# Second MLP of a linear-attention and two-MLP kernel as Strassen block products over three parts of 768 tokens

## The chip, the cores and the metric

The kernel runs on one core of a Trainium2 chip. The metric is the device time of one execution in microseconds, on that core. The time before is the median of three executions, 895.91 us (895.73 to 897.20).

## What is computed

Linear attention over 4 batches of 8 heads and 576 positions, then two MLPs over the 2304 tokens that result. The second MLP adds no bias and has no scale; its activation is Mish.

```python
def _attn_ref(q, k, v):
    q_s = softmax of q over the head dimension (64)
    k_s = softmax of k over the sequence (576)
    kv = np.einsum('bhsd,bhse->bhde', k_s, v)
    return np.einsum('bhsd,bhde->bhse', q_s, kv)

x = attention output as [2304, 512]
h = x @ w_in;  r = np.maximum(h, 0.0);  g = s * (r * r) + b;  x = g @ w_out      # first MLP, [512, 2048], [2048, 512]
h = x @ w_in;  g = h * np.tanh(softplus(h));  out = g @ w_out                    # second MLP, same sizes
```

All inputs are 32-bit floats to the reference; on the chip the four weight matrices arrive as 64-bit floats, two 32-bit words per element, and the kernel makes 32-bit floats of them with shifts and masks.

## The kernel before, in words

Every product of the MLPs is made to near 32-bit precision by three passes of the matmul unit: each operand is split into a high part (rounded to the matmul's format) and a low part (the rest), and `passes` (L177 to L185, matmul L181) adds high x high, high x low and low x high in PSUM. The high part is a copy on ACT (L174, or L160 for weights), the low part a subtraction on DVE (`minus`, L171).

The tokens are cut into five chunks of 512, 256, 512, 512 and 512 (`CHUNKS`). One *step* is one chunk and one block f of 128 of the 2048 columns: `emit_h` makes h (128 hidden columns x the chunk, 4 blocks of the 512 inputs x 3 passes = 12 matmuls), `emit_relu2` (first MLP) or `emit_mish` (second) makes g and its split, `emit_y` adds the block's share of y (12 matmuls in a chunk of 512). Steps 0 to 79 are the first MLP (called MLP1 here), steps 80 to 159 the second (MLP2), whose chunks come in the order 0, 2, 1, 3, 4. h runs two steps ahead of y in MLP1 and three in MLP2 (`LEAD`, `LEAD2`, `h_slot`). In the first MLP y lies as output columns x tokens, in the second as tokens x output columns. At the end of a chunk `y_out` scales y and stores it, in MLP1 to `y_dram` in DRAM (tile `yd`, L300) and in MLP2 to the output. `x2_load` (L215) reads a chunk back as input of MLP2, and `x_split` adds the bias term `bsum` (L205, L206).

Beside these steps run the attention of the next chunk (the `att` stages, placed by `at` at step numbers) and the conversion of the weights. A *unit* holds 1024 elements per partition: `load_w` (L112, L117) brings 1 MB of raw words in two DMAs, `conv_abs`, `conv_bits` (L137 to L151), `conv_hi` (L160) and `conv_lo` make its two halves. The units of MLP1 are converted at the start and in the first chunk; those of MLP2 from step 61 on, on the fly, into the slots that MLP1 gives up. SP issues nearly all DMAs and does so strictly in its order: a DMA that waits holds the ones behind it. The tile framework orders each engine's instructions by program order and priorities; `order` rows below show the result.

Of the kernel before, what the change touches and what calls it, by code (L numbers as in the profile page):

```python
# [26 lines left out]
def kernel(  # L27
# [169 lines left out]
    def x_split(ph, c, kk):  # L197
# [3 lines left out]
        if ph == 0:  # L201
            split(hi, lo, src)
        else:
            b = bsum[:, kk:kk + 1]
            nc.scalar.activation(out=hi, in_=src, func=AF.Identity, bias=b)  # L205
            nc.vector.scalar_tensor_tensor(  # L206
                out=lo, in0=src, scalar=b, in1=hi.bitcast(F32), op0=ALU.add, op1=ALU.subtract
            )
# [2 lines left out]
    def x2_load(c):
        n = CHUNKS[c]
        for kk in range(NK):
            t = xp.tile([P, CM], F32, tag=f"xn{kk}", name=f"x2_{c}_{kk}")
            nc.sync.dma_start(out=t[:, 0:n], in_=y_dram[c][:, kk, :])  # L215
            x_next[1, c, kk] = t[:, 0:n]
# [521 lines left out]
```

## Time and profile before

| | |
|---|---|
| median of 3 executions | 895.91 us (895.73 to 897.20) |
| profiled execution | 896.14 us |
| its span, first to last instruction | 894.4 us |
| mean granted clock of the matmul unit | 0.988 of 2.4 GHz |
| matmul unit (PE) | 859.6 us busy, 4364 matmuls, as many weight loads |
| DVE, ACT, POOL | 392.3, 389.9, 3.7 us busy |
| bytes moved by DMA | 62.59 MB |

The profiled execution is 1.74 us longer than its span, and 0.23 us above the median. An engine is busy in a stretch when one of its instructions runs; a wait is put down to the instruction whose end released it. DMA issues are not counted as busy time.

### The profile page before, as it was taken

To read this page: it belongs to the slowest core of one execution; us is meant where nothing else is said; L and a number is where in the kernel's file an instruction comes from. 1 tells how busy PE (TensorE), PEld (TensorE's weight loads), DVE (VectorE), ACT (ScalarE), POOL (GpSimd) and SP (SyncE) were. 2 spreads that over 40 slices of the span, in tenths; PEclk is the share of its full clock that TensorE was granted. 3 is DMA by queue.
4 is the path that set the end of the run, shared out by engine and by line. 5 is a ranking of instruction groups with operands and counts; after the bars stand their busy time and mean duration, and the time that the engine had idled before them with its cause. 6 is when DMAs were issued, how large, how long until landed. Compare 5 with 4: busy or idle time off the path is not lost.

```text
span 894.4 us, 11164 instructions
## 1 busy us (share of the span) xinstructions
PE 859.6 (96%) x4364; PEld 713.1 (80%) x4364; DVE 392.3 (44%) x648; ACT 389.9 (44%) x901; POOL 3.7 (0%) x26
## 2 busy tenths in 40 slices
PE   5689987999999999999999999999999999999998
PEld 3368876998788888888888888888889888888886
DVE  5999856445333444344787497211111211121111
ACT  7677656477555645444346233322122321132221
POOL 1000000000000000000000000000000000000000
PEclk9899997999999999999999999999999999999999
DMA  8982231322111011014444151010011100001001
GB/s 239 288 289 67 80 85 39 100 64 59 43 39 39 12 47 24 1 50 139 141 143 167 68 186 49 25 48 0 1 48 48 41 31 1 0 1 48 1 1 47
DMA packets 72516, 62.59 MB, mean 70 GB/s; under 512 B 39312, under 2 KB 62096, under 8 KB 72464
## 3 DMA queue, kind: packets, MB, share of 16 engines
q1 hardware_dynamic: 71376, 60.84, 21.9%
q10 hardware_dynamic: 1088, 1.05, 0.4%
q8 instruction: 34, 0.56, 0.3%
q14 instruction: 18, 0.15, 0.1%
HBM read 52.43 MB, written 9.44 MB: 69 GB/s over the span
## 4 chain that ended last, share of the span: by engine, by line
PE 90%; DMA 4%; SPq 2%; ACT 1%; DVE 1%; issue 0%; DVEq 0%; ACTq 0%
PE h L181 43%; PE y L181 43%; DMA raw<-in_moe_w_out_dram 3%; PE x L181 1%; PE kv L463 1%; DMA q<-in_q_dram 1%; PE qt L472 1%; DMA kvb<-in_k_dram 1%; SPq L112 1%; SPq L342 0%; SPq L370 0%; ACT q L428 0%; PE km L404 0%; PE km L397 0%; SPq L346 0%
## 5 line engine op out<-in xcount | busy, mean ns | idle before, releaser
L181 PE MATMUL h<-xh,w 128*128 128x512 f32 (+1 forms) x1280 | 390.7, 372 | 10.6 <-ACT w L160 5.0
L181 PEld LDWEIGHTS h<-xh,w 128*128 128x128 f32 x1280 | 235.5, 190 | 53.8 <-ACT w L160 5.6
L171 DVE TENSOR_TENSOR gl<-r,gh 128x512 fp32r<-128x512 f32 (+1 forms) x159 | 100.8, 635 | 353.2 <-ACT r L255 265.4
L181 PE MATMUL h<-xl,w 128*128 128x512 f32 (+1 forms) x640 | 237.4, 371 | 0.5 <-DVE xl L171 0.4
L181 PE MATMUL y<-gh,w 128*128 128x512 f32 (+1 forms) x640 | 196.5, 372 | 0.0
L181 PE MATMUL y<-w,gh 128*128 128x512 f32 x568 | 175.0, 390 | 0.0
L254 ACT ACTIVATE gh<-h 128x512 fp32r<-128x512 f32 (+1 forms) x79 | 43.8, 554 | 253.5 <-PE y L181 228.3
L181 PEld LDWEIGHTS h<-xl,w 128*128 128x128 f32 x640 | 121.5, 190 | 23.3 <-DVE xl L171 2.8
L181 PEld LDWEIGHTS y<-gh,w 128*128 128x128 f32 x640 | 117.4, 189 | 19.7
L181 PEld LDWEIGHTS y<-w,gh 128*128 128x128 f32 x568 | 105.6, 188 | 21.0
L181 PE MATMUL y<-gl,w 128*128 128x512 f32 (+1 forms) x320 | 119.9, 375 | 0.0
L181 PE MATMUL y<-w,gl 128*128 128x512 f32 x284 | 110.3, 389 | 0.0
L245 ACT ACTIVATE r<-h 128x512 f32<-128x512 f32 (+1 forms) x80 | 44.3, 553 | 103.9 <-PE h L181 95.7
L181 PEld LDWEIGHTS y<-gl,w 128*128 128x128 f32 x320 | 60.9, 190 | 10.6 <-DVE gl L171 0.4
L181 PEld LDWEIGHTS y<-w,gl 128*128 128x128 f32 x284 | 53.4, 188 | 11.3
L428 ACT ACTIVATE q<-q,qm 128x64 f32<-128x64 f32 x144 | 48.2, 336 | 18.1 <-DVE qm L409 17.9
L160 ACT CAST w<-t 128x1024 fp32r<-128x1024 f32 (+1 forms) x34 | 34.0, 1001 | 47.6 <-DVE t L151 46.2
L174 ACT CAST gh<-r 128x512 fp32r<-128x512 f32 (+1 forms) x80 | 46.0, 577 | 3.8 <-PE y L181 2.0
L246 ACT ACTIVATE r<-r 128x512 f32<-128x512 f32 (+1 forms) x80 | 46.8, 589 | 1.9
L255 ACT ACTIVATE r<-h 128x512 f32<-128x512 f32 (+1 forms) x80 | 44.0, 551 | 0.0
L171 DVE TENSOR_TENSOR w<-t,w 128x1024 fp32r<-128x1024 f32 (+1 forms) x34 | 39.2, 1153 | 2.9 <-ACT w L160 2.9
L151 DVE SCALAR_TENSOR_TENSOR t<-raw,t 128x1024 int32<-128x1024 int32 (+1 forms) x34 | 39.2, 1153 | 0.1
(96 smaller groups left out, 514.4 us busy)
## 6 DMA issues: line engine op xcount, KB each, us to landing
raw<-in_moe_w_in_dram SPq DMA_DIRECT2D x32, 512.0 KB, 4.6
raw<-in_moe_w_out_dram SPq DMA_DIRECT2D x32, 512.0 KB, 5.6
out_dram<-ys SPq DMA_DIRECT2D x17, 256.0 KB, 2.4
yd<-ys SPq DMA_DIRECT2D x16, 256.0 KB, 2.1
x<-yd SPq DMA_DIRECT2D x16, 256.0 KB, 3.5
kb<-in_k_dram SPq DMA_DIRECT2D x12, 256.0 KB, 3.0
vb<-in_v_dram SPq DMA_DIRECT2D x24, 128.0 KB, 2.8
kvb<-in_k_dram SPq DMA_DIRECT2D x4, 256.0 KB, 3.8
```

Source lines behind the costliest of these rows:

```text
L112: nc.sync.dma_start(out=part.rearrange("p (k f) -> p k f", k=NK), in_=src[:, 2 * f * P:2 * (f + 1) * P].rearrange("(k p) f -> p k f", p=P),)
L151: nc.vector.scalar_tensor_tensor(out=w_t[u], in0=w_raw[u][:, :, 0], scalar=29, in1=w_t[u], op0=ALU.logical_shift_right, op1=ALU.bitwise_or,)
L160: nc.scalar.copy(out=hi, in_=w_t[ph, u].bitcast(F32))
L171: eng.tensor_tensor(out=lo, in0=src, in1=hi.bitcast(F32), op=ALU.subtract)
L174: nc.scalar.copy(out=hi, in_=src)
L181: mm = nc.tensor.matmul(out=ps, lhsT=x, rhs=y, start=start, stop=stop)
L245: nc.scalar.activation(out=r, in_=h_ps.pop(m), func=AF.Relu)
L246: nc.scalar.activation(out=r, in_=r, func=AF.Square)
L254: nc.scalar.activation(out=hi, in_=h_ps[m], func=AF.Mish)
L255: nc.scalar.activation(out=r, in_=h_ps.pop(m), func=AF.Mish)
L428: nc.scalar.activation(out=t[:, i // rq, i % rq], in_=t[:, i // rq, i % rq], func=AF.Exp, bias=mx[:, i], accum_out=sm[:, i])
L463: nc.tensor.matmul(out=ps[h * D:(h + 1) * D, 0:D + 1], lhsT=ke[:, r, h], rhs=vb[:, r, h * (D + 1):(h + 1) * (D + 1)], start=(r == 0), stop ...
```

## The change

MLP2 is written anew; MLP1 and the attention keep their steps. The three passes stay.

- **Products.** The tokens are taken in three parts of 768 (`PARTS`). For h, the 512 inputs are halved, the hidden columns are halved (1024 and 1024, block i paired with block i + 8), and the 768 tokens are halved (384): a 2x2 block product, made by seven block products and sums and differences of blocks (Winograd's form of Strassen's scheme) instead of eight. The same is done for y: 2048 inputs halved, 512 output columns halved (256), tokens halved. So h has, per part and i, 7 products x 2 blocks x 3 passes = 42 matmuls with 384 columns, and y, per part, 7 products x 8 i x 3 token blocks x 3 passes = 504 matmuls with 256 columns.
- **Weight operands.** A *prep unit* i brings two raw blocks (1 MB in two DMAs), makes 32-bit floats of them (L265 on ACT, L266 to L279 on DVE), four sums or differences (L285), splits blocks and sums (casts L302, differences L285) and stores them to DRAM in four DMAs of 512 KB (L315). Eight units of w_in run at steps 18 to 61, eight of w_out at steps 62 to 79, the latter alternately in the buffers of pool `convert` (four, shared with the stores of y) and of `convert2` (four).
- **Streaming.** In MLP2 all weight operands come back from DRAM in every part, through a ring of 9 tiles of 512 KB: per i of h three tiles and a half (L796), per product of y four (L844), 168 tiles' worth in all.
- **Inputs.** Per part eight DMAs (L749) bring x, ACT adds the bias (L752), `x_ops` makes the block sums and splits the seven operands (22 instructions on DVE and 14 on ACT per part).
- **Sums behind products.** In h, DVE adds products, ACT applies Mish, DVE makes the sums of g; in y, each g operand is split just before its product, and sums of y blocks stay in SBUF tiles until they are stored (L831).
- **Memory.** All pools of MLP1 are closed before those of MLP2 are opened; the ring, x and PSUM tiles of MLP2 lie where tiles of MLP1 lay. `convert` has four buffers in place of three, `r` one in place of two.

```diff
-ORDER2 = (0, 2, 1, 3, 4)
+PARTS = (((0, 0, 512), (1, 0, 256)), ((2, 0, 512), (3, 0, 256)), ((3, 256, 512), (4, 0, 512)))
...
-    LEAD2 = 3
+    HC = 384
+    HD = DM // 2
...
-    cv = ctx.enter_context(tc.tile_pool(name="convert", bufs=3))
+    cv = ctx.enter_context(tc.tile_pool(name="convert", bufs=4))
...
-    rp = ctx.enter_context(tc.tile_pool(name="r", bufs=2))
+    rp = one.enter_context(tc.tile_pool(name="r", bufs=1))
...
+    wi_d = [dram.tile([P, 4, 2, DM], F32, name=f"wi_d{i}") for i in range(NF // 2)]
+    wo_d = [dram.tile([P, 8, 2, 2, HD], F32, name=f"wo_d{i}") for i in range(NF // 4)]
...
-        at(L0 + s - 3, "load", load_w, *u)
-        at(L0 + s - 1, "abs", conv_abs, *u)
-        at(L0 + s - 1, "bits", conv_bits, u)
-        at(L0 + s, "hi", conv_hi, *u)
-        at(L0 + s, "lo", conv_lo, *u)
+    END = (NC - 1) * NF - 3
+    pools = {}
+    for i in range(NF // 2):
+        s = (18, 25, 32, 37, 42, 48, 53, 58)[i]
+        at(s, "load", lambda i: prep_load("wi", i, cv), i)
+        at(s + 1, "prep", prep_bits, "wi", i)
+        at(s + 2, "prep", prep_sums, "wi", i)
+        at(s + 3, "prep", prep_out, "wi", i)
+        s = END + 1 + 2 * i
+        at(s, "load", lambda i: prep_load("wo", i, pools[i % 2]), i)
+        at(s + 1, "prep", prep_bits, "wo", i)
+        at(s + 2, "prep", prep_sums, "wo", i)
+        at(s + 3, "prep", prep_out, "wo", i)
...
+    for n in range(NS, NS + 8):
+        run(n, "prep")
+    one.close()
+    cv2.close()
...
+    def x_load(sc):
+        xf = []
+        for kk in range(NK):
+            t = st.tile([P, 2 * HC], F32, tag="s1", bufs=4, name=f"xf{sc}_{kk}")
+            o = 0
+            for c, a, b in PARTS[sc]:
+                nc.sync.dma_start(out=t[:, o:o + b - a], in_=y_dram[c][:, kk, a:b])
+                o += b - a
+            nc.scalar.activation(out=t, in_=t, func=AF.Identity, bias=bsum[:, kk:kk + 1])
+            xf.append(t)
+        return xf
+    def x_ops(sc, xf):
+        for p in range(1, 8):
+            xo[p] = halves(st.tile([P, 4 * HC], F32R, tag=f"xo{p}", name=f"xo{sc}_{p}"))
+        for j in range(2):
+            o = slice(j * HC, (j + 1) * HC)
+            b11, b12 = xf[j][:, 0:HC], xf[j][:, HC:2 * HC]
+            b21, b22 = xf[2 + j][:, 0:HC], xf[2 + j][:, HC:2 * HC]
+            t1, t2, t3, t4 = (st.tile([P, HC], F32, tag="c", bufs=5, name=f"t{n}_{sc}") for n in range(4))
+            tt(t1, b12, b11, ALU.subtract)
+            tt(t3, b22, b12, ALU.subtract)
+            tt(t2, b22, t1, ALU.subtract)
+            tt(t4, b21, t2, ALU.subtract)
+            for p, b in ((1, b11), (2, b21), (6, t2), (5, t1), (7, t3), (3, b22), (4, t4)):
+                split(xo[p][0][:, o], xo[p][1][:, o], b)
+    def product(w, o, p):
+        ps = bank()
+        wh, wl = halves(w)
+        for kk in range(2):
+            a = slice(o + kk * P, o + (kk + 1) * P)
+            b = slice(kk * HC, (kk + 1) * HC)
+            passes(ps[:, 0:HC], (wh[:, a], wl[:, a]), (xo[p][0][:, b], xo[p][1][:, b]), kk == 0, kk == 1)
+        return ps[:, 0:HC]
...
+    for sc in range(len(PARTS)):
+        if sc == 0:
+            xf = x_load(sc)
+            x_ops(sc, xf)
+        g11, g12, g21, g22, s1, op = {}, {}, {}, {}, {}, {}
+        for i in range(N2):
+            w = [ring() for _ in range(4)]
+            for piece, t in enumerate(w):
+                o = slice(HD if piece == 3 else 0, DM)
+                nc.sync.dma_start(
+                    out=t.rearrange("p (n d) -> p n d", n=2)[:, :, o].bitcast(F32), in_=wi_d[i][:, piece, :, o]
+                )
...
+            def c_block(t, a, ps):
+                tt(t, a, ps, ALU.add)
+                nc.scalar.activation(out=t, in_=t, func=AF.Mish)
+            nc.scalar.copy(out=u2, in_=product(w[0], 0, 1))
+            c_block(g11[i], u2, product(w[0], HD, 2))
+            tt(u2, u2, product(w[1], 0, 6), ALU.add)
+            op[i] = g_split(g11[i])
+            tt(u3, u2, product(w[1], HD, 7), ALU.add)
+            p5 = product(w[2], 0, 5)
+            c_block(g22[i], u3, p5)
+            tt(u2, u2, p5, ALU.add)
+            c_block(g21[i], u2, product(w[2], HD, 3))
+            c_block(g12[i], u3, product(w[3], HD, 4))
+            if i % 2 == 0:
+                s1p = st.tile([P, 2 * HC], F32, tag="s1", bufs=4, name=f"s1_{sc}_{i}")
+            s1[i] = s1p[:, i % 2 * HC:(i % 2 + 1) * HC]
+            tt(s1[i], g21[i], g22[i], ALU.add)
+            tt(g21[i], g11[i], g21[i], ALU.subtract)
+            tt(g11[i], s1[i], g11[i], ALU.subtract)
...
+        u2, u3 = [], []
+        for p, src, j in ((1, None, 0), (2, g12, 2), (6, g11, 5), (7, g21, 6), (5, s1, 4), (3, g12, 3), (4, g22, 7)):
+            banks = [bank()[:, 0:HD] for m in range(3)]
+            a = []
+            w = []
+            for i in range(N2):
+                if i % 2 == 0:
+                    t = ring()
+                    nc.sync.dma_start(out=t.bitcast(F32), in_=wo_d[i // 2][:, j].rearrange("p a b c -> p (a b c)"))
+                    t = t.rearrange("p (a b c) -> p a b c", a=2, b=2)
+                w.append((t[:, i % 2, 0], t[:, i % 2, 1]))
+                a.append(op[i] if p == 1 else g_split(src[i]))
+                if p == 2:
+                    tt(g12[i], g12[i], g11[i], ALU.subtract)
+            tail = sc == len(PARTS) - 1 and p == 4
+            order = [(i, m) for i in range(N2) for m in range(3)]
+            if tail:
+                order.sort(key=lambda im: im[1])
+            for i, m in order:
+                o = slice(m * P, (m + 1) * P)
+                ps = banks[m]
+                passes(ps, (a[i][0][:, o], a[i][1][:, o]), w[i], i == 0, i == N2 - 1)
+                if i < N2 - 1:
+                    continue
+                if p == 1:
+                    u2.append(evt())
+                    nc.scalar.copy(out=u2[m], in_=ps)
+                elif p == 2:
+                    t = evt()
+                    tt(t, u2[m], ps, ALU.add)
+                    store(t, 0, m, 0)
...
+            if p == 5 and sc + 1 < len(PARTS):
+                xf = x_load(sc + 1)
+            if p == 3 and sc + 1 < len(PARTS):
+                x_ops(sc + 1, xf)
```

PE at the end of MLP1, before. `y_64` are the four output blocks of the last chunk, `h_4454` and `h_4473` the first two h of MLP2:

```order
L181 MATMUL y_64_3893<-gh_4364,w_16_1318 128x512
L181 MATMUL y_64_3893<-gl_4365,w_16_1318 128x512
L181 MATMUL y_64_3893<-gh_4364,w_16_1318 128x512
L181 MATMUL h_4454<-xh_0_0_4426,w_0_3908 128x512 [waits Activation_49]
L181 MATMUL h_4454<-xl_0_0_4427,w_0_3908 128x512 [waits DVE_49]
L181 MATMUL h_4454<-xh_0_0_4426,w_0_3908 128x512
L181 MATMUL h_4454<-xh_0_1_4430,w_0_3908 128x512 [waits Activation_49]
L181 MATMUL h_4454<-xl_0_1_4431,w_0_3908 128x512 [waits DVE_49]
L181 MATMUL h_4454<-xh_0_1_4430,w_0_3908 128x512
```

The matmuls of MLP2 follow on those of MLP1; their x and weights are another chunk's, loaded long ahead. With the change, in the same place (`p` are products, `xo_1` the operand of product 1, `ring` a weight tile):

```order
L182 MATMUL y_64_4113<-gh_4692,w_16_1330 128x512
L182 MATMUL y_64_4114<-gl_4693,w_16_1330 128x512
L182 MATMUL y_64_4114<-gh_4692,w_16_1330 128x512
L182 MATMUL p<-xo_1_4806,ring 128x384 [waits DMAHW2_49,Activation_49]
L182 MATMUL p<-xo_1_4806,ring 128x384 [waits DVE_49]
L182 MATMUL p<-xo_1_4806,ring 128x384
L182 MATMUL p<-xo_1_4806,ring 128x384 [waits Activation_49]
L182 MATMUL p<-xo_1_4806,ring 128x384 [waits DVE_49]
L182 MATMUL p<-xo_1_4806,ring 128x384
L182 MATMUL p<-xo_2_4807,ring 128x384 [waits Activation_49]
L182 MATMUL p<-xo_2_4807,ring 128x384 [waits DVE_49]
```

The last matmul of MLP1 is followed by product 1 of the first i, which needs x and the first ring tile; no matmul of MLP2 stands ahead of it.

SP at that place, before: `yd` are the stores of the last chunk's y, `x_2` the input loads for the second chunk of MLP2.

```order
L215 DMA x_2_0_4588<-yd_91 128x512 [waits DVE_49]
L215 DMA x_2_1_4590<-yd_91 128x512 [waits DVE_49]
L215 DMA x_2_2_4592<-yd_91 128x512 [waits DVE_49]
L215 DMA x_2_3_4594<-yd_91 128x512 [waits DVE_49]
L300 DMA yd_93<-ys_79_4532 128x512 [waits DMAHW4_49,Activation_49]
L300 DMA yd_93<-ys_79_4535 128x512 [waits DMAHW5_49,DVE_49]
L300 DMA yd_93<-ys_79_4538 128x512 [waits DMAHW6_49,Activation_49]
L300 DMA yd_93<-ys_79_4541 128x512 [waits DMAHW7_49,DVE_49]
L112 DMA raw_12_4633<-in_moe_w_in_dram 128x4x256 [waits DMAHW0_49,DVE_49]
```

With the change (`xf` are the loads of x, `ring` the first weight tile of h; just ahead stand the store of the first output block, L245, and the last store of the last prep unit, L315):

```order
L749 DMA xf_0_4790<-yd_89 128x512 [waits DMAHW7_49,PE_49]
L749 DMA xf_0_4790<-yd_90 128x256 [waits DMAHW0_49]
L749 DMA xf_1_4794<-yd_89 128x512 [waits DMAHW1_49]
L245 DMA yd_93<-ys_79_4758 128x512 [waits DMAHW2_49,DVE_49]
L749 DMA xf_1_4794<-yd_90 128x256 [waits DMAHW3_49]
L749 DMA xf_2_4798<-yd_89 128x512 [waits DMAHW4_49]
L245 DMA yd_93<-ys_79_4761 128x512 [waits DMAHW5_49,Activation_49]
L749 DMA xf_2_4798<-yd_90 128x256 [waits DMAHW6_49]
L245 DMA yd_93<-ys_79_4764 128x512 [waits DMAHW7_49,DVE_49]
L749 DMA xf_3_4802<-yd_89 128x512 [waits DMAHW0_49]
L749 DMA xf_3_4802<-yd_90 128x256 [waits DMAHW1_49]
L796 DMA ring<-wi_d_94 128x1024 [waits DMAHW2_49]
```

The loads of x stand behind and between the stores of the last y, and the first ring tile stands behind the last of them, though the data they read were stored many steps before.

DVE at the end of MLP1, with the change (`gl_4693` is the low part of g for step 79, `t_wo`, `s_wo` and `r_wo` the tiles of the last prep unit):

```order
L269 TENSOR_SCALAR t_wo_4587<-t_wo_4587 128x1024 [waits DVE_49]
L274 SCALAR_TENSOR_TENSOR t_wo_4587<-r_wo_4583,t_wo_4587 128x512 [waits DMAHW7_49,DVE_49]
L274 SCALAR_TENSOR_TENSOR t_wo_4587<-r_wo_4584,t_wo_4587 128x512 [waits DMAHW1_49]
L279 SCALAR_TENSOR_TENSOR t_wo_4587<-r_wo_4583,t_wo_4587 128x512 [waits DVE_49]
L279 SCALAR_TENSOR_TENSOR t_wo_4587<-r_wo_4584,t_wo_4587 128x512 [waits DVE_49]
L172 TENSOR_TENSOR gl_4693<-r_4694,gh_4692 128x512 [waits PE_49,Activation_49]
L285 TENSOR_TENSOR s_wo_4588<-t_wo_4587 128x256 [waits DMAHW0_49,DVE_49]
L285 TENSOR_TENSOR s_wo_4588<-t_wo_4587 128x256 [waits DVE_49]
L285 TENSOR_TENSOR s_wo_4588<-t_wo_4587,s_wo_4588 128x256 [waits DVE_49] x2
L285 TENSOR_TENSOR t_wo_4587<-t_wo_4587,r_wo_4583 128x1024 [waits DVE_49,Activation_49]
L285 TENSOR_TENSOR s_wo_4588<-s_wo_4588,r_wo_4584 128x1024 [waits Activation_49]
L240 TENSOR_SCALAR ys_79_4758<-y_64_4112,sb_s 128x512 [waits DMAHW3_49,DMAHW5_49,DVE_49,PE_49]
```

The shifts and masks of the last unit stand ahead of `gl_4693`, its sums and differences behind it and ahead of the first scaling of y.

## Rows read from the trace of the kernel before

**Rows 1.** The page, parts 1 and 4: the whole execution.

```profile
PE 859.6 (96%) x4364; PEld 713.1 (80%) x4364; DVE 392.3 (44%) x648; ACT 389.9 (44%) x901; POOL 3.7 (0%) x26
...
PE 90%; DMA 4%; SPq 2%; ACT 1%; DVE 1%; issue 0%; DVEq 0%; ACTq 0%
```

**Rows 2.** Busy us by stretch: PE, PEld, DVE, ACT, POOL, PEclk, DMA share, GB/s.

```profile
30.00:60.00 30.00, 21.03 (x89) 13.86 (x88) 27.78 (x44) 20.28 (x43) 0.00 (x0) 0.88 1.03 348
130.00:150.00 20.00, 12.35 (x61) 9.87 (x61) 15.12 (x27) 13.10 (x46) 0.00 (x0) 0.74 0.20 47
150.00:420.00 270.00, 269.56 (x1562) 228.72 (x1562) 110.56 (x221) 147.36 (x393) 0.00 (x0) 1.00 0.18 47
420.00:497.00 77.00, 77.00 (x340) 63.46 (x339) 57.74 (x72) 36.48 (x54) 0.00 (x0) 1.00 0.45 151
...
650.00:890.50 240.50, 240.44 (x1150) 202.46 (x1148) 42.00 (x69) 59.27 (x121) 0.00 (x0) 1.00 0.06 21
```

**Rows 3.** Groups of instructions by form, PE alone, from 497.4 to 890.45.

```profile
L181 PE MATMUL y<-w,gh 128*128 128x512 f32 x568 | 175.0, 390 | 0.0
L181 PE MATMUL h<-xh,w 128*128 128x512 f32 x504 | 163.8, 389 | 0.0
L181 PE MATMUL y<-w,gl 128*128 128x512 f32 x284 | 110.3, 389 | 0.0
L181 PE MATMUL h<-xl,w 128*128 128x512 f32 x252 | 97.9, 389 | 0.0
L181 PE MATMUL h<-xh,w 128*128 128x256 f32 x128 | 25.2, 282 | 0.0
L181 PE MATMUL h<-xl,w 128*128 128x256 f32 x64 | 18.1, 283 | 0.0
```

**Rows 4.** Chain of waits, end of MLP1: start, us, what.

```profile
494.47 8.16 PE h L181 x36
```

**Rows 5.** Chain of waits, a stretch with the chunk of 256 tokens.

```profile
198.23 1.44 PE y L181 x12
```

**Rows 6.** Timeline of PE, attention output (x<-): start, length of each.

```profile
205.06 0.34 PE L181 MATMUL x<-qth,kvl 128*128 128x384 f32 x1
205.24 0.22 PE L181 MATMUL x<-qth,kvh 128*128 128x128 f32 x1
205.31 0.27 PE L181 MATMUL x<-qtl,kvh 128*128 128x128 f32 x1
```

**Rows 7.** Groups by form, DVE and ACT: busy, mean ns, idle before.

```profile
L171 DVE TENSOR_TENSOR gl<-r,gh 128x512 fp32r<-128x512 f32 x127 | 87.3, 689 | 309.3 <-ACT r L255 229.4 <-ACT gh L174 79.9
...
L171 DVE TENSOR_TENSOR w<-t,w 128x1024 fp32r<-128x1024 f32 x30 | 36.5, 1215 | 2.2 <-ACT w L160 2.2
...
L160 ACT CAST w<-t 128x1024 fp32r<-128x1024 f32 x30 | 31.5, 1051 | 45.2 <-DVE t L151 43.9 <-DVE qs L439 0.8 <-DVE qs L440 0.4
...
L137 DVE TENSOR_SCALAR t<-t 128x1024 f32<-128x1024 f32 x30 | 20.5, 687 | 2.9 <-ACT t L129 2.5
...
L129 ACT ACTIVATE t<-raw 128x1024 f32<-128x1024 f32 x15 | 17.0, 1140 | 7.5 <-DMA raw<-in_moe_w_out_dram 4.1 <-DVE w L171 1.7 <-DVE rs L491 1.6
L171 DVE TENSOR_TENSOR gl<-r,gh 128x256 fp32r<-128x256 f32 x32 | 13.5, 422 | 43.9 <-ACT r L255 36.1 <-ACT gh L174 7.0 <-PE h L181 0.8
...
L146 DVE SCALAR_TENSOR_TENSOR t<-raw,t 128x512 int32<-128x512 int32 x4 | 2.7, 683 | 0.0
```

**Rows 8.** The page, part 6: DMA issues, KB each, us to landing.

```profile
raw<-in_moe_w_in_dram SPq DMA_DIRECT2D x32, 512.0 KB, 4.6
raw<-in_moe_w_out_dram SPq DMA_DIRECT2D x32, 512.0 KB, 5.6
out_dram<-ys SPq DMA_DIRECT2D x17, 256.0 KB, 2.4
```

**Rows 9.** Timeline of SP, issues of DMAs.

```profile
420.67 0.50 SPq L117 DMA_DIRECT2D raw<-in_moe_w_out_dram  x1
...
572.94 2.31 SPq L215 DMA_DIRECT2D x<-yd  x4
```

**Rows 10.** Timeline of PE around the idle time after 131 us.

```profile
137.25 1.35 PE L463 MATMUL kv<-vb,ke 128*64 128x65 f32 x20 [5.69 <-ACT ke L436]
...
141.18 0.79 PE L181 MATMUL h<-xh,w 128*128 128x512 f32 x1 [1.95 <-ACT w L160]
...
142.20 0.63 PE L181 MATMUL y<-gh,w 128*128 128x512 f32 x1
142.62 0.63 PE L181 MATMUL y<-gl,w 128*128 128x512 f32 x1
...
146.77 0.39 PE L181 MATMUL h<-xl,w 128*128 128x512 f32 x1
```

**Rows 11.** Chain of waits, the last pieces.

```profile
876.85 13.61 PE y L181 x60
...
890.54 0.38 ACT ys L287
...
890.94 0.42 DVE ys L287
```

More of the change, by code (lines that the diff above doesn't have):

```diff
@@ L200, in x_split @@
         hi, lo = (t[:, 0:n] for t in x_tiles(kk, f"{ph}_{c}_{kk}"))
[L201 to L208, printed above, removed]
-        x_t[ph, c, kk] = (hi, lo)
[L211 to L216, printed above, removed]
+        split(hi, lo, src)
+        x_t[ph, c, kk] = (hi, lo)
     def emit_h(m, kks=None):
@@ new lines, in emit_y, with y_out @@
+            passes(y_ps[c][m][:, 0:nt], (wh[:, o], wl[:, o]), g_t[n], f == 0, f == NF - 1)
+    def y_out(n):
+        c = steps[n][1]
+        nt = CHUNKS[c]
+        for m, ps in enumerate(y_ps.pop(c)):
+            ys = cv.tile([P, 2 * DM], F32, tag="t", name=f"ys{m}_{n}")[:, 0:nt]
+            if m % 2:
+                nc.vector.tensor_scalar(
+                    out=ys, in0=ps[:, 0:nt], scalar1=sb_s, scalar2=None, op0=ALU.mult
+                )
+            else:
+                nc.scalar.activation(out=ys, in_=ps[:, 0:nt], func=AF.Copy, scale=sb_s)
+            nc.sync.dma_start(out=y_dram[c][:, m, :], in_=ys)
@@ new lines, with prep_load @@
+    wi_d = [dram.tile([P, 4, 2, DM], F32, name=f"wi_d{i}") for i in range(NF // 2)]
+    wo_d = [dram.tile([P, 8, 2, 2, HD], F32, name=f"wo_d{i}") for i in range(NF // 4)]
+    prep = {}
+    def prep_load(z, i, pool):
+        r = [pool.tile([P, 2 * DM], I32, tag="t", name=f"r{j}_{z}{i}") for j in range(2)]
+        for j in range(2):
+            load_raw(1, z, i + j * NF // 2, r[j])
+        t, s = (pool.tile([P, 2 * DM], F32, tag="t", name=f"{a}_{z}{i}") for a in "ts")
+        prep[z, i] = (r, t, s)
@@ new lines, in prep_out @@
+    def prep_out(z, i):
+        r, t, s = prep.pop((z, i))
+        for a, src in zip(r, (t, s)):
+            tt(src.bitcast(F32R), src, a.bitcast(F32), ALU.subtract)
+        for part, blocks, sums in ((0, r[0], r[1]), (1, t, s)):
+            for j, a in enumerate((blocks, sums)):
+                a = a.bitcast(F32)
+                if z == "wi":
+                    to = wi_d[i][:, 0::3] if j == 0 else wi_d[i][:, 1:3]
+                    nc.sync.dma_start(out=to[:, :, part], in_=a.rearrange("p (n w) -> p n w", n=2))
+                else:
+                    nc.sync.dma_start(
+                        out=wo_d[i // 2][:, 4 * j:4 * j + 4, i % 2, part],
+                        in_=a.rearrange("p (n w) -> p n w", n=4),
+                    )
@@ L671 @@
         emit_relu2(m)
-    for n in range(2 * NS):
+    for n in range(NS):
         ph, c, f = steps[n]
-        if n == (NC - 1) * NF - 3:
+        if n == END:
             att.close()
-            mp["raw"] = ctx.enter_context(tc.tile_pool(name="raw", bufs=2))
-        hs = h_slot.get(n, ())
-        boundary = any(steps[m][2] == 0 for m in hs)
+            cv2 = ExitStack()
+            pools[0], pools[1] = cv, cv2.enter_context(
+                tc.tile_pool(name="convert2", bufs=4, side="right", reuse_waits="tile")
+            )
+        m = n + LEAD
+        boundary = m < NS and steps[m][2] == 0
         run(n, "att5", "att2", "att3")
```

232 lines of the change are left out of this document (122 added, 110 removed).

## The prediction

> **What bounds the kernel now.** I read the page first. PE is busy for 96% of the span and makes 90% of the chain that ended last, DVE and ACT are below half [rows 1]: the kernel is bound by the matmul unit, and only matmuls removed, or PE idle time made, move the end. The table by stretch shows where: from 150 us on PE has no idle time to speak of at full granted clock, while DMA is nearly unused behind 650 us (21 GB/s) [rows 2]. So MLP2 costs what its matmuls cost. The groups of that stretch count them [rows 3]: 864 of y (852 in the two groups, 12 under another name) and 768 of h with 512 columns (756 recorded), 192 of h with 256. Busy means there (389 ns) are pipelined lengths and can't be added; the pitch is what counts. The chain gives it: 36 matmuls of 512 columns in 8.16 us, 0.2267 us each [rows 4]; 12 of 256 in 1.44 us, 0.120 each [rows 5]. One of 384 lasts from 205.06 to 205.24 and one of 128 from 205.24 to 205.31 [rows 6]; with two decimals that is too coarse, so I put 384 halfway between 256 and 512: 0.1733.
>
> MLP2 before is then 768 x 0.2267 + 192 x 0.120 + 864 x 0.2267 = 174.1 + 23.0 + 195.9 = 393.0 us. The last matmul ends at 876.85 + 13.61 = 890.46 [rows 11], so MLP1 and the attention hold PE until 497.4, and 3.9 us follow the last matmul.
>
> **Matmuls.** After: h 3 parts x 8 i x 42 = 1008 x 0.1733 = 174.7; y 3 x 504 = 1512 x 0.120 = 181.4; together 356.1 us, **36.9 less**. An eighth of 393.0 would be 49.1; the other 12 are the price of shorter matmuls, since 0.120 is more than half of 0.2267. Every one has its own weight load, as before. These 256-column rows ran with a load before each, so loads don't stretch them.
>
> **Joint between the MLPs.** Before, there was none: h of MLP2 follows y of MLP1 in PE's order. Now product 1 does, and its inputs are requested late. Call T the end of the last MLP1 matmul. In SP's order the first ring tile is 14th, counted from the store of the first y block; that store can go at about T - 0.6 (its matmuls end six pitches, 1.4 us, before T, and its scaling takes some 0.7). An issue takes 0.50 to 0.58 us (2.31 / 4) [rows 9], so the tile is issued at about T + 6.9 and, at the 4.6 us of a 512 KB load [rows 8], is there at T + 11.5. The x loads are earlier in the queue, and the first operands need two loads, bias and a split: T + 8 or so, hidden by the tile. DVE's 22 instructions of `x_ops` (0.555 each, halfway between 0.422 and 0.689 [rows 7]) take 12.2 us, and the later products follow them at PE's pace. So PE idles 11.5 us. What an idle PE costs besides is in rows 10: after 5.69 and 1.95 us of idle time a matmul of 512 columns came each 0.43 us (142.20 to 142.62), which is the 1.2 GHz level, from 141.18 until about 146.2: 5.0 us at half rate, 2.5 lost. **Joint: +14.0 us.** Bounds: 8.8, if issues take 0.50, the tile lands like a store of 256 KB, in 2.4 [rows 8], and nothing is lost at half rate (14 x 0.50 - 0.6 + 2.4); 20, if the last prep unit, whose store stands between, has to wait another 5.6 us for raw words [rows 8].
>
> **Prep units.** One costs DVE 2 x 0.687 + 4 x 0.683 + 4 x 0.422 + 2 x 1.215 = 8.2 us, ACT 2 x 0.66 (an estimate, 0.58 of the 1.140 at 1024) + 2 x 1.051 = 3.4 [rows 7]; sixteen are 131 and 55 us. The first eight fall between 150 and 420 us, where DVE is 41% and ACT 55% busy [rows 2]: 8 x 8.2 on top of 110.6 of 270 us is hidden. The last eight have 18 steps of 24 x 0.2267 = 5.44 us, 98 us, and replace conversions that made DVE 75% busy there with PE at 100% [rows 2]; DVE then needs 66 + 18 x 0.69 + some 6 = 84 of 98 us. They move 8 x 3 MB = 25 MB, 257 GB/s, where that stretch had 151 [rows 2]. A unit of pool `convert` is a chain: loads 6, ACT 1.3, DVE 4.1, 1.7, casts 2.1, 2.4, stores about 3, together 20.6 us, against the 21.8 (four steps) until the next one wants its buffers. That is tight, its shifts stand ahead of `gl` in DVE's order, and h runs only two steps ahead of y. I take **+6 us** here; bounds 0 and 28 (the 25 MB at 200 GB/s take 126 us, not 98).
>
> **Start.** `convert` with four buffers and `r` with one shift ACT's and DVE's order in the first 60 us, when DVE is 28 of 30 us busy [rows 2]. The nearest row for what such a shift is worth is the stretch from 130 to 150 us, where PE lacks 7.65 us because a weight was converted late [rows 2, 10]: bounds -7.6 (that wait vanishes) and +7.6 (another like it). I take **+2**, since more conversions now stand ahead of the first h.
>
> **Inside MLP2.** In h, DVE has 11 instructions of 0.555 per i, 6.1 us, against 42 x 0.1733 = 7.3 of PE. In y, per part, 48 low parts (26.6), 8 sums (4.4), 21 evictions at 0.42 (8.8) and 22 of `x_ops` (12.2): 52 of 60.5 us. Enough, but `x_ops` crowds into the last products of a part. I take **+5 us** for two crossings between parts and the first of each phase; bounds 0 and 17 (a DVE instruction of 384 at the full 0.689 adds 3 x (8 x 0.3) + 3 x 3 in the two phases).
>
> **End.** The last eviction has 256 columns (0.42), then an issue (0.50 [rows 9]) and a landing (2.4 [rows 8]): 3.3 in place of 3.9.
>
> **Sum.** 497.4 + 2 + 6 + 14.0 + 356.1 + 5 + 3.3 = 883.8 as span; 1.74 us lie around it: 885.5 against the 896.14 of the profiled execution, 10.6 less. The median is 0.23 below that execution, so the forecast is **885.3 us**.
>
> [...]
>
> **Rival 1, the stream sets the pace (0.07).** 168 tiles of 512 KB (88 MB) must come in 356 us, one in 2.12. A load takes 4.6 us from issue to landing [rows 8], so at least 2.2 have to be under way at once. If waits for ring buffers leave two, MLP2 takes 168 x 2.3 = 386 us, 30 more: 916 us, **slower than before**. For it: SP's order puts stores and x loads, with waits for DVE, between tiles. Against: at 30 to 60 us loads of the same size moved 348 GB/s [rows 2], one per 1.5 us, and nine ring tiles run about 19 us ahead. [...]
>
> **Rival 2, preparation starves MLP1 (0.20).** The chain of a `convert` unit decides: above 21.8 us each of its four units comes later, and since ACT and DVE run in order, the g of MLP1 waits behind. At 28 us per unit that is 4 x 6 = 25 us in place of my 6: 905 us, slower, too. For: 257 GB/s beside PE. Against: the stretch from 420 us, where DVE already waited for such loads, has no PE idle time [rows 2].
>
> **Rival 3, the joint is short (0.12).** With the joint at its lower bound of 8.8 and no stall in preparation or inside MLP2: 885.3 - 5.2 - 6 - 5 = 869 us. For: PE without idle time from 150 us on [rows 2], so well ordered that it may stay so. Against: SP's order at the joint, which no priority can shorten below its issues.
>
> **Chances.** My case 0.60, own range 875 to 896. A change within 0.2% (1.8 us) can't be told from none. Faster: 0.55 of the 0.60, 0.12, and 0.08 from a mild rival 2: 0.75. Same: 0.05. Slower: 0.20. The range from 867 to 907 leaves out rival 1, the worst half of rival 2 and a corner below: not quite 0.2.
>
> **What would show it.** Right: 2520 matmuls of MLP2 at 0.173 and 0.120 us pitch; an idle stretch of PE of 9 to 13 us near 505 us released by the ring tile's DMA, with the granted clock at half behind it; DMA near 250 GB/s until the end; small gaps of 1 to 3 us at the two crossings. Wrong: PE idle time between 415 and 505 us released by ACT or DVE that waited for raw w_out loads (rival 2); PE waiting for ring tiles throughout, and a DMA share near 1 (rival 1); no gap at the joint (rival 3).

## The result, and the profile after

The changed kernel takes 876.03 us (median of 4, 875.59 to 876.67) against 895.82 us before (median of 4): ratio 0.9778, interval 0.9761 to 0.9794. It is faster by 19.8 us, 2.2%. I had forecast 885.3, so the sign and the range held, but the gain is nearly double the 10.6 us of the forecast. The sum was 9.3 us too high: its term for the joint was too low, and those for the start, the preparation and the stalls inside MLP2 were too high.

The page of the kernel after, parts 1 and 4, which answer to [rows 1]:

```profile
PE 824.6 (94%) x5060; PEld 741.9 (85%) x5060; DVE 630.7 (72%) x1190; ACT 498.0 (57%) x1109; POOL 3.7 (0%) x26
...
PE 79%; DMA 8%; DVE 5%; ACT 3%; SPq 3%; issue 2%; DVEq 0%; ACTq 0%
PE p L182 41%; PE y L182 17%; PE h L182 17%; DMA raw<-in_moe_w_out_dram 2%; DMA r_wo<-in_moe_w_out_dram 2%; DMA q<-in_q_dram 1%; PE x L182 1%; DMA yd<-ys 1%; SPq L388 1%; ACT q L446 1%; PE kv L481 1%; DMA wo_d<-r_wo 1%; ACT r_wo L302 1%; PE qt L490 1%; DVE t L152 1%
```

PE is 35 us less busy, DVE at 72% where it had 44%; the chain is still one of matmuls, but only 79% of it, with DMA and DVE behind. The stretches, as in [rows 2] (busy us of PE, PEld, DVE, ACT, POOL, granted clock, DMA share, GB/s):

```profile
0.00:60.00 60.00, 35.06 (x180) 22.87 (x181) 49.09 (x94) 42.01 (x122) 3.67 (x26) 0.80 0.93 291
...
130.00:150.00 20.00, 20.00 (x119) 16.86 (x118) 12.47 (x25) 13.16 (x38) 0.00 (x0) 1.00 0.17 44
...
420.00:497.00 77.00, 74.04 (x326) 60.66 (x324) 59.18 (x95) 43.60 (x65) 0.00 (x0) 1.00 0.73 244
497.00:520.00 23.00, 7.59 (x34) 7.62 (x35) 12.80 (x25) 12.60 (x22) 0.00 (x0) 0.63 1.02 349
520.00:580.00 60.00, 60.00 (x368) 60.00 (x367) 50.45 (x99) 26.80 (x54) 0.00 (x0) 1.00 0.84 272
580.00:640.00 60.00, 60.00 (x484) 60.00 (x484) 43.78 (x95) 31.57 (x67) 0.00 (x0) 1.00 0.88 282
```

The stretch from 130 to 150 us has lost its idle time, the joint (497 to 520) has gained one, and MLP2 runs without a gap at full clock beside 272 to 282 GB/s. The waits of PE from 420 us to the end:

```profile
PE p L182 <- DMA ring<-wi_d: 17.6, 1, 17.6
PE y L182 <- DVE gl L172: 0.7, 1, 0.7
```

One wait of 17.6 us is nearly all. The timeline of PE has its end, and the first part of h and of y (start, length):

```profile
512.41 7.80 PE L182 MATMUL p<-xo,ring 128*128 128x384 f32 x34 [17.63 <-DMA ring<-wi_d]
...
519.70 52.85 PE L182 MATMUL p<-xo,ring 128*128 128x384 f32 x304
572.39 52.71 PE L182 MATMUL p<-ring,op 128*128 128x256 f32 x438
```

The chain that ended last has the pace of y at the end of the kernel (start, us, what):

```profile
849.92 20.53 PE p L182 x171
...
870.47 0.42 DVE d L285
```

304 matmuls of 384 columns between 519.70 and 572.39 us are 0.1733 each, and 171 of 256 columns in 20.53 us are 0.120 each, as in [rows 5]. From these rows: MLP1 ends at 512.41 - 17.63 = 494.8 us, MLP2 lasts from 512.41 to 870.45, 358.0 us, and 3.3 us follow. Against the kernel before MLP2 is 35.0 us shorter, MLP1 ends 2.6 us earlier, and the joint takes 17.6 us of that back. What made the joint that long stands in the chain of waits (start, us, what):

```profile
479.76 7.59 DMA r_wo<-in_moe_w_out_dram
...
487.37 0.67 ACT t_wo L265
...
492.04 1.06 ACT r_wo L302
...
493.12 2.90 DMA wo_d<-r_wo
...
496.12 0.70 ACT ys L244
...
496.83 3.65 DMA yd<-ys
...
500.61 0.66 DVE ys L240
501.27 5.67 DMA yd<-ys
...
506.96 5.31 DMA ring<-wi_d
```

The raw words of the last w_out unit land only at 487.4, 7.4 us before MLP1 ends. Its casts and stores hold the buffers in which y is scaled (496.12), the stores of y follow, and the first ring tile goes out at 506.96 when one of these stores, eight DMAs ahead of it, has landed: 12.2 us behind the last matmul where I had 6.9. That last wait alone is 0.3 us, since SP is busy with the loads of x until 506.6. The first store of y goes out 2.7 us later than I had put it, the thirteen DMAs from there to the ring tile take 10.1 us and not 7.5, and from its issue to the first matmul pass 5.5 us, not 4.6.

### The profile page after: what moved, and what is told of

It reads as the page before. It is cut to its first block, busy times and chain, and to the rows that moved or that the text cites. A ratio compares the mean times of both kernels' runs of the same rounds, so it can differ in the third digit from the quotient of the medians.

```text
span 873.8 us, 14203 instructions
## 1 busy us (share of the span) xinstructions
PE 824.6 (94%) x5060; PEld 741.9 (85%) x5060; DVE 630.7 (72%) x1190; ACT 498.0 (57%) x1109; POOL 3.7 (0%) x26
## 4 chain that ended last, share of the span: by engine, by line
PE 79%; DMA 8%; DVE 5%; ACT 3%; SPq 3%; issue 2%; DVEq 0%; ACTq 0%
PE p L182 41%; PE y L182 17%; PE h L182 17%; DMA raw<-in_moe_w_out_dram 2%; DMA r_wo<-in_moe_w_out_dram 2%; DMA q<-in_q_dram 1%; PE x L182 1%; DMA yd<-ys 1%; SPq L388 1%; ACT q L446 1%; PE kv L481 1%; DMA wo_d<-r_wo 1%; ACT r_wo L302 1%; PE qt L490 1%; DVE t L152 1%
## 5 line engine op out<-in xcount | busy, mean ns | idle before, releaser
L182 PE MATMUL h<-xh,w 128*128 128x512 f32 (+1 forms) x640 | 202.2, 380 | 6.2 <-ACT w L161 3.7
L182 PE MATMUL p<-xo,ring 128*128 128x384 f32 x1008 | 177.3, 336 | 17.6 <-DMA ring<-wi_d 17.6
L182 PEld LDWEIGHTS p<-xo,ring 128*128 128x128 f32 x1008 | 176.2, 189 | 18.0 <-ACT xo L175 18.0
L182 PE MATMUL p<-ring,op 128*128 128x256 f32 x1512 | 182.2, 283 | 0.0
L182 PEld LDWEIGHTS p<-ring,op 128*128 128x128 f32 x1512 | 182.0, 192 | 0.0
L182 PEld LDWEIGHTS h<-xh,w 128*128 128x128 f32 x640 | 119.7, 193 | 29.5 <-ACT xh L175 4.2
L182 PE MATMUL h<-xl,w 128*128 128x512 f32 (+1 forms) x320 | 120.9, 379 | 3.2 <-DVE xl L172 3.2
L175 ACT CAST op<-g 128x384 fp32r<-128x384 f32 x144 | 72.2, 511 | 44.7 <-PE p L182 43.9
L172 DVE TENSOR_TENSOR op<-g,op 128x384 fp32r<-128x384 f32 x144 | 78.4, 553 | 25.6 <-ACT op L175 24.3
L182 PEld LDWEIGHTS h<-xl,w 128*128 128x128 f32 x320 | 62.0, 194 | 14.5 <-DVE xl L172 4.3
L182 PEld LDWEIGHTS y<-gl,w 128*128 128x128 f32 x320 | 60.2, 188 | 12.2 <-DVE gl L172 2.5
L285 DVE TENSOR_TENSOR g<-u,p 128x384 f32<-128x384 f32 x96 | 52.5, 552 | 10.9 <-PE p L182 8.6
L446 ACT ACTIVATE q<-q,qm 128x64 f32<-128x64 f32 x144 | 48.2, 336 | 10.7 <-DVE qm L427 10.4
L285 DVE TENSOR_TENSOR u<-u,p 128x384 f32<-128x384 f32 x72 | 39.7, 551 | 20.0 <-PE p L182 19.8
```

What stands on the lines that cost most here:

```text
L172: eng.tensor_tensor(out=lo, in0=src, in1=hi.bitcast(F32), op=ALU.subtract)
L175: nc.scalar.copy(out=hi, in_=src)
L182: mm = nc.tensor.matmul(out=ps, lhsT=x, rhs=y, start=start, stop=stop)
L285: nc.vector.tensor_tensor(out=out, in0=a, in1=b, op=op)
L446: nc.scalar.activation(out=t[:, i // rq, i % rq], in_=t[:, i // rq, i % rq], func=AF.Exp, bias=mx[:, i], accum_out=sm[:, i])
```

## The experiments

Single runs stand beside runs of the kernel before on the same chip (896.69, 894.97 and 895.17 us in the three sets). MLP1's end is read as the start of the first product less PE's wait there.

**Why MLP1 got shorter.** Its steps were not changed, but two pools were. One buffer for r:

```diff
-    rp = ctx.enter_context(tc.tile_pool(name="r", bufs=2))
+    rp = ctx.enter_context(tc.tile_pool(name="r", bufs=1))
```

> The kernel before with one r buffer in place of two. The PE idle time of the stretch from 130 to 150 us (7.65 us, and 2.5 us at the 1.2 GHz level behind it) is gone after the change, though MLP1 itself was not meant to change. Theory A (the fourth convert buffer lets conversions run ahead and takes that wait away): r alone does nothing good, PE idle time of 130 to 150 us stays at 6 to 8 us, time 895 to 899. Theory B (r's single buffer reorders ACT so that the late weight is converted sooner): the idle time is under 2 us and the time is 885 to 890.

Measured: 885.46 us, 11.2 less than before, by a pool size alone, as theory B had it. And with the fourth convert buffer beside it:

```diff
-    cv = ctx.enter_context(tc.tile_pool(name="convert", bufs=3))
+    cv = ctx.enter_context(tc.tile_pool(name="convert", bufs=4))
```

> The kernel before with four convert buffers and one r buffer (a fourth without this does not fit). Theory A: PE has no idle time from 130 to 150 us, the first 60 us cost 2 to 3 us more PE time as they do after the change, time 887 to 891. Theory C (the wait went because the conversions of the second MLP left the program, whatever the buffers): the idle time stays and the time is 894 to 899.

Measured: 890.98. The time fell in theory A's interval, but the first run had already refuted A: r takes the wait away, and the fourth buffer costs 5.5 us. Theory C falls too, since the conversions of MLP2 are still in this program. The stretches, with r alone and with both:

```profile
0.00:60.00 60.00, 38.81 (x202) 25.43 (x203) 46.64 (x93) 41.25 (x123) 3.67 (x26) 0.89 0.93 282
...
130.00:150.00 20.00, 19.18 (x121) 15.96 (x119) 15.63 (x30) 16.16 (x44) 0.00 (x0) 1.00 0.30 82
```

```profile
0.00:60.00 60.00, 35.69 (x178) 23.22 (x179) 48.30 (x93) 41.77 (x122) 3.67 (x26) 0.80 0.94 287
...
130.00:150.00 20.00, 20.00 (x117) 16.77 (x116) 13.37 (x26) 13.65 (x40) 0.00 (x0) 1.00 0.18 44
```

Both have PE at full clock from 130 to 150 us, and busy but for 0.8 us with r alone; the fourth buffer takes 3 us of PE work and clock (0.89 to 0.80) out of the first 60. Seven executions of the kernel before, in the third set, lie between 893.4 and 898.5 us, so 5.5 us between two single runs would not be sure by the time alone. The matmuls counted in the first 60 us bear it out: 177 to 180 in all six kernels with four convert buffers, 198 to 210 in all seven with three.

What r changes stands in the timelines of SP and ACT. Before (one line), and with one r:

```profile
124.95 0.55 SPq L112 DMA_DIRECT2D raw<-in_moe_w_in_dram  x1
```

```profile
85.57 0.60 ACT L245 ACTIVATE r<-h 128x512 f32<-128x512 f32 x1 [2.02 <-DVE gl L171]
...
118.91 0.52 SPq L112 DMA_DIRECT2D raw<-in_moe_w_in_dram  x1
```

With one r the relu of a step waits until DVE has made the low part of the step before, and the loads of the weight that was late in [rows 10] go out at 118.9 us, not 124.95. By which of the moved instructions these loads come 6 us earlier was not tested, nor why the order in the first 60 us is worse with four buffers. The changed kernel with two r buffers was not run: that r does the same there is carried over from these two runs, the second of which has nearly its row from 130 to 150 us.

In the changed kernel, three convert buffers again, and the fourth tile of a prep unit in a pool of its own:

```diff
-    cv = ctx.enter_context(tc.tile_pool(name="convert", bufs=4))
+    cv = ctx.enter_context(tc.tile_pool(name="convert", bufs=3))
+    cvs = ctx.enter_context(tc.tile_pool(name="convert_s", bufs=1))
...
-        t, s = (pool.tile([P, 2 * DM], F32, tag="t", name=f"{a}_{z}{i}") for a in "ts")
+        t = pool.tile([P, 2 * DM], F32, tag="t", name=f"t_{z}{i}")
+        s = (cvs if pool is cv else pool).tile([P, 2 * DM], F32, tag="t", name=f"s_{z}{i}")
```

> The changed kernel with three convert buffers as before and the fourth tile of a prep unit in a pool of its own, so that the conversions of the first MLP run no further ahead than before. Before with r single and three convert buffers took 885.46 us, with four 890.98. If the fourth buffer is what makes the start longer after the change: PE idle time of the first 60 us as in the run with r single, MLP1's end 4 to 6 us earlier, time 870 to 873. If the w_out chain at the end holds MLP1 back anyway: the gain at the start comes out again as idle time behind 420 us, 874 to 877.

Measured: 866.42, better than expected. MLP1 ends at 489.2, 5.6 us earlier, about the 5.5 of the pair above; and the joint is 14.1 us in place of 17.6: the raw words of the last w_out unit land 10.7 us before MLP1 ends, not 7.4. Whether the earlier start or the unit's separate buffer brought them forward was not separated.

**What makes the joint.** First the buffers of the last y:

```diff
-            ys = cv.tile([P, 2 * DM], F32, tag="t", name=f"ys{m}_{n}")[:, 0:nt]
+            ys = (pools[1] if n == NS - 1 else cv).tile([P, 2 * DM], F32, tag="t", name=f"ys{m}_{n}")[:, 0:nt]
```

> The changed kernel with the last chunk's y scaled into buffers of convert2, which are free, not of convert, where the last prep unit's stores hold them. Theory D (the joint of 17.6 us is long because y's scaling waits for those buffers, and SP's order passes that on to the first ring tile): the joint shrinks by 2 to 5 us, time 871 to 874. Theory E (SP's own issues and the wait of each DMA for the one eight before it set the tile's time): joint within 1.5 us of 17.6, time 875 to 877.

Measured: 875.97, joint 17.3, as theory E had it: theory D falls. The timeline of SP shows why:

```profile
497.64 1.13 SPq L315 DMA_DIRECT2D wo_d<-s_wo  x1
498.87 2.99 SPq L245 DMA_DIRECT2D yd<-ys  x3
501.95 4.16 SPq L749 DMA_DIRECT2D xf<-yd  x8
506.82 5.78 SPq L796 DMA_DIRECT2D ring<-wi_d  x9
```

The unit's last stores still stand in SP's queue ahead of the stores of y (all but the first of them), these ahead of x, and the ring tile goes out behind them all, again at 506.8, after 0.7 us of waiting for an x load to land. So it is the place of the late unit in SP's queue that counts, and the buffers alone do not. Next, x and two i of ring tiles from POOL's empty queue:

```diff
-                nc.sync.dma_start(out=t[:, o:o + b - a], in_=y_dram[c][:, kk, a:b])
+                (nc.gpsimd if sc == 0 else nc.sync).dma_start(out=t[:, o:o + b - a], in_=y_dram[c][:, kk, a:b])
...
-                nc.sync.dma_start(
+                (nc.gpsimd if sc == 0 and i < 2 else nc.sync).dma_start(
```

> The changed kernel with the x loads of the first part and its first eight ring tiles issued by POOL, whose queue is empty, not behind SP's stores. If SP's order is what makes the joint (my prediction's reading): the tile is there before the last matmul of MLP1, the joint falls to 3 to 8 us (what remains is bias and split of the first operand on ACT and DVE), the time at half clock shrinks with it, time 859 to 868. If memory or ACT and DVE hold the first product back instead: joint over 10 us, time 870 or more.

Measured: 881.76, 5.7 us worse than the changed kernel. The tiles came early, and the price was elsewhere. The waits of PE, the chain, and the timeline of ACT:

```profile
PE y L182 <- ACT gh L175: 10.4, 1, 10.4
PE p L182 <- ACT xo L175: 7.5, 2, 7.1
```

```profile
476.46 11.62 DMA wo_d<-r_wo
...
488.14 11.21 DMA r_wo<-in_moe_w_out_dram
```

```profile
496.58 0.66 ACT L265 ACTIVATE t_wo<-r_wo 128x512 f32<-128x512 f32 x1 [16.07 <-DMA r_wo<-in_moe_w_out_dram]
```

POOL's sixteen loads went out from 472 to 484 us, in the middle of w_out's preparation: one store of it took 11.6 us (3.0 is the median after), its two raw loads 16.6 and 11.2. ACT stood at the first raw words for 16.1 us (until 496.58), and the g of MLP1's last step but one stood behind them: 10.4 us of idle PE inside MLP1. This is my rival 2 in small. But PE's waits from 420 us on add up to 18.4 us here and to 18.3 in the changed kernel, so idle time was only moved. Most of what the run lost is clock: PE works at half clock behind both waits, for some 4 and 9 us, where the changed kernel has 3.6 (512.4 to 516):

```profile
498.00:502.00 4.00, 3.54 (x8) 2.53 (x9) 2.54 (x4) 2.81 (x5) 0.00 (x0) 0.50 0.02 6
513.90:522.90 9.00, 8.23 (x19) 5.48 (x20) 7.87 (x18) 7.34 (x14) 0.00 (x0) 0.50 0.41 127
```

To move the tiles without this, the last unit had to go:

```diff
+            if sc == 0 and i == 1:
+                prep_load("wo", LATE, cv)
+            elif sc == 0 and 2 <= i < 5:
+                (prep_bits, prep_sums, prep_out)[i - 2]("wo", LATE)
```

(with `LATE = 6` left out of the units at steps 62 to 79, beside the three convert buffers).

> The same, and the last w_out unit on the convert buffers (unit 6) is prepared during i = 1 to 4 of the first part's h, ahead of its first use in y. If that unit's chain makes the joint long (its raw words late, y's scaling behind its stores): the joint falls from 17.6 to about the 11.5 us of SP's issues and one landing, the idle time between 420 and 497 us (3 us) goes, time 860 to 866. If the joint is only SP's order: joint 16 us or more, time 869 or more. A new wait of the 4th ring tile of y's first product for this unit's stores would show as PE idle time near 570 us.

Measured: 863.24. The joint is 11.3 us, near the 11.5 that the prediction had worked out for SP's order without a late unit; that is in part luck, since the tile goes out earlier than in that sum (5.2 us behind the last matmul, not 6.9) and takes longer to land (5.9 us, not 4.6):

```profile
486.35 0.70 ACT ys L245
...
487.06 2.05 DMA yd<-ys
...
489.29 0.76 DVE ys L241
...
492.97 5.90 DMA ring<-wi_d
...
499.00 21.00 PE p L183 x104
```

With the x loads on POOL beside it:

```diff
-                nc.sync.dma_start(out=t[:, o:o + b - a], in_=y_dram[c][:, kk, a:b])
+                (nc.gpsimd if sc == 0 else nc.sync).dma_start(out=t[:, o:o + b - a], in_=y_dram[c][:, kk, a:b])
```

> The same, and the x loads of the first part (1.5 MB) issued by POOL, ring tiles by SP as ever. When x and sixteen tiles' worth went out early, the unit then under way lost its bandwidth and MLP1 stalled; with that unit moved and only 1.5 MB early, the joint should lose the eight issues of SP ahead of the ring tile (4.4 us): joint 6 to 9 us, time 855 to 862. If the early loads again hurt w_out's preparation: PE idle time behind 450 us and a time over the run without POOL.

Measured: 872.29, a miss. PE started after 5.6 us, as expected, and then stopped:

```profile
PE p L183 <- ACT xo L176: 11.2, 1, 11.2
PE p L183 <- DMA ring<-wi_d: 5.6, 1, 5.6
```

```profile
504.45 0.66 ACT L267 ACTIVATE t_wo<-r_wo 128x512 f32<-128x512 f32 x1 [10.88 <-DMA r_wo<-in_moe_w_out_dram]
...
506.24 0.93 ACT L757 ACTIVATE xf<-xf,bsum 128x768 f32<-128x768 f32 x1
```

ACT's order had the late unit's first instructions, which wait for raw words, ahead of the bias of the later x blocks. With these pinned behind the activations of i = 2:

```diff
-            nc.scalar.activation(out=t[:, o], in_=a[:, :, 1].bitcast(F32), func=AF.Abs)
+            act = nc.scalar.activation(out=t[:, o], in_=a[:, :, 1].bitcast(F32), func=AF.Abs)
+            if (z, i) == ("wo", 6):
+                tc.keep_in_program_order(act)
```

> The run with the x loads on POOL, and ACT's first two instructions of the late w_out unit pinned behind the activations of i = 2. There, PE started after 5.6 us and then waited 11.2 us more, since ACT had that unit's raw words ahead of the later x biases. If that order is all: one PE wait of 5 to 7 us at the joint for the first ring tile, none behind it, 854 to 859 us. If the late unit's 3 MB beside the stream is what hurts: PE waits remain behind the first product and the time stays over 862.

Measured: 857.45 us, ratio to before 0.9581, interval 0.9547 to 0.9615: the best version, 18.6 us below the changed kernel. PE waits 5.7 us at the joint, now for the bias of x on ACT, and 0.7 us for a ring tile. The four tiles of the first i on POOL too:

```diff
-                nc.sync.dma_start(
+                (nc.gpsimd if sc == 0 and i == 0 else nc.sync).dma_start(
```

> The same, with the four ring tiles of the first i on POOL too, behind the x loads and so ahead of MLP1's end. If nothing but late requests makes the joint, it falls to 1 to 4 us (PE then waits for bias and split of the first operand at most) and the time to 850 to 856; the clock may then stay at 2.4 GHz. If the 1.9 MB more slow the last w_out stores and raw loads as in the run with sixteen early loads: PE idle time ahead of the joint, and a time over the other's.

Measured: 859.66, ratio 0.9601 (0.9572 to 0.9630): a miss, and not better than the other. The waits at the joint are 2.2 and 1.6 us, in four pieces, 2.6 us less than there, but the half clock lasts longer. The stretch at half clock in the run before this one, and in this one:

```profile
491.70:495.00 3.30, 3.30 (x10) 3.30 (x11) 3.30 (x8) 3.30 (x8) 0.00 (x0) 0.50 0.98 369
```

```profile
492.70:502.30 9.60, 8.68 (x23) 6.24 (x23) 8.50 (x19) 7.46 (x15) 0.00 (x0) 0.50 0.93 343
```

From the end of MLP1 to the last matmul this run takes 365.8 us, the other 364.6. The other 3 us between the two profiled executions lie ahead of MLP1's end, with a granted clock of 0.83 against 0.91 in the first 60 us, and the executions of the two versions overlap (858.70 to 861.57 and 855.96 to 859.37). Less idle time at the joint gained nothing once the time at half clock grew with it.

**How far the stream is from the bound.** A smaller ring:

```diff
-    RING = 9
+    RING = 5
```

> The changed kernel with a ring of 5 tiles, not 9. Theory of my rival 1 (the stream is near to setting the pace): PE waits for ring tiles all through the second MLP and the time rises by 15 us or more, over 890. My reading (the stream has room: 0.85 share and no PE wait with nine): five tiles are still 10 us ahead, twice the 4.6 us of a load, and the time stays within 3 us of 876.

Measured: 879.73. 3.7 us more, a little over what was expected. PE waits for ring tiles at the joint (17.1 us) and 0.4 us elsewhere, so the stream is not the cause. 1.8 us of it lie ahead of MLP1's end, whose order moved with the pools (PE 355.20 us busy from 60 to 420, 357.45 after the change); behind the joint PE is at half clock for 5.4 us and not 3.6, and waits 0.7 us for a split on DVE. And every tile loaded twice:

```diff
-                nc.sync.dma_start(
+                for _ in range(2):
+                    nc.sync.dma_start(
...
```

(and the same at L844; only bytes are added.)

> The changed kernel with every ring tile loaded twice, 176 MB in place of 88 in the second MLP. This measures how near rival 1 is: the stream is then the bound, and its rate is what the DMA engines give. At the 348 GB/s of the start of the kernel before: 506 us in place of 358, so about 1024 us in all; at 300 GB/s 1105; if loads hide behind PE even so (a rate of 490 GB/s), 876.

Measured: 981.37. Then the stream is the bound, with the DMA engines busy throughout at 400 GB/s, more than I had expected from 348:

```profile
520.00:970.00 450.00, 381.45 (x2471) 363.31 (x2472) 270.97 (x536) 169.31 (x334) 0.00 (x0) 0.96 1.03 400
```

```profile
ring<-wo_d SPq DMA_DIRECT2D x168, 512.0 KB, 9.2
```

A load lands in 9.2 us and PE waits for tiles in both phases. The changed kernel asks for 266 GB/s: two thirds.

## Why the prediction was right, and where it was off

Against the profiled execution, term by term (span 873.8, forecast 883.8; the four differences add up to the 10.0 but for rounding):

| term | forecast | measured |
|---|---|---|
| MLP1's end: 497.4, start +2, preparation +6 | 505.4 | 494.8 |
| PE idle at the joint | 11.5 | 17.6 |
| MLP2: 356.1, half clock 2.5, stalls 5 | 363.6 | 358.0 |
| behind the last matmul | 3.3 | 3.3 |

- **Matmuls: right, and the greater part of the gain.** 356.1 us from pitches of 0.1733 and 0.120, both as measured, and about 2 lost at half rate make the 358.0. The 0.1733 had been put halfway between two rows. The price of shorter matmuls, 12 of the ideal 49 us, is real.
- **"Start +2": the step that failed.** I had named the idle time at 130 to 150 us as the nearest row and let it vanish only as a bound, -7.6. It vanished. The runs on the kernel before share it out: r single -10.7 us of span, the fourth buffer +5.5, together -5.2 where I took +2. That the first 60 us would get worse was right, but it was mis-sized. I treated pool sizes as details; one of them was worth as much as half of the whole gain.
- **"Preparation +6": too dear.** PE lost 2.0 us from 212 to 330 and 0.7 behind 420. The chain of the convert units was late, as worked out (tight against 21.8 us), but the lateness ended in the joint, not in MLP1.
- **"Joint 14.0": too cheap.** SP's order was the right mechanism: with the late unit taken away, 11.3 us against 11.5. What I missed is that the last unit is late and its stores hold back y, x and the ring tile in SP's queue, priced only in the upper bound of 20, that an issue of SP waits here for the DMA eight ahead of it (the last store of y 0.7 us, the ring tile 0.3), and that the tile takes 5.3 us to land and not 4.6, beside 349 GB/s (497 to 520): together 6.1 us more. Half clock behind the wait: 0.50 from 512 to 516 us, 1.8 us lost where I had 2.5.
- **"Inside MLP2 +5": nothing.** DVE is 76% busy there and nowhere on the chain; the crossings between parts cost no idle time.
- **Luck.** The joint, too cheap by 6.1 us, hid part of what the other terms had too dear (16.2 us); without that the time would lie below my own range of 875 to 896.
- **Two bounds** were added up wrongly, without effect on the forecast: the joint's lower one counts 14 issues where the sum counts 13 (8.3 us, not 8.8), and the upper one inside MLP2 comes to 16.2 us, not 17.
- **Rivals.** The stream (rival 1) was a third short of its bound (266 of 400 GB/s). Preparation starving MLP1 (rival 2) didn't come in this kernel, and came at once, 10.4 us, when other loads were put beside it. The joint was not short (rival 3), and became so in the best version.

## What to carry to other kernels

When a change resizes buffer pools, an unchanged stage is a term of its own: find its idle stretches first and ask which of them hang on the order of two engines, since they may vanish (7.65 us here) or come anew. Where two phases meet, follow each queue's order through the joint with everything that is late in it (14.1 us of joint with the late unit, 11.3 without); loads that could go early cost what the transfers beside them lose (a store of w_out took 11.6 us and not 3.0), so move the late work first and the early loads after. Count a wait together with the time at half clock behind it: the early loads from POOL lost 5.7 us with the idle time of PE from 420 us on all but unchanged (18.4 us, 18.3 without them), and some 13 us at half clock in place of 3.6. A stream's distance from its bound can be measured by loading everything twice (400 GB/s here, against the 266 asked for).

## What the runs showed of the hardware

- Loads of 512 KB came at 400 GB/s for 450 us when every tile was loaded twice, at 9.2 us each; by these two figures some seven were under way (an estimate). In the changed kernel, where they hide behind PE, they come at 266 GB/s in 4.6 us.
- Matmuls of 256 columns, each with its own weight load, held 0.120 us for hundreds in a row (438 in 52.71 us), PE and PEld both busy throughout (60.00 of 60.00 us from 580 to 640), which no row before had shown for so long. The pitches of 256, 384 and 512 columns (0.120, 0.1733, 0.2267) lie on one line, 13 ns and 0.417 ns a column, so nothing shows that the load stretches the shortest of them more than the others. That is 2.40 columns a nanosecond at a granted clock of 1.00, and 512 columns each 0.43 us are about 1.2 at 0.50 [rows 10]: the 2.4 and 1.2 GHz named elsewhere stand for these rates, and of the clock itself the runs show the granted share alone.
- How long PE ran at half clock (0.50) did not go by the length of the wait. It was 3.6 us after 17.6 us of idle time in the changed kernel (granted clock 0.50 until 516 us and 0.98 behind it), 5.0 us after the 5.69 and 1.95 us of [rows 10], 5.9 us after 11.3 us without the late unit, 3.3 us after 5.7 us in the best version, and 9.6 us in the run after it, where four waits together made 3.8 us.
